# Reordering the first four steps and joining the weights' pieces one step later, in a fused Mamba-2 and cosine-gated feed-forward kernel

## The chip, the cores and the metric

The kernel runs on one core of a Trainium2 chip. The metric is the device time of one execution in microseconds (us), as a median over runs. The program works with five engines: TensorE (PE, matmuls), VectorE (DVE), ScalarE (ACT), GpSimd (POOL) and SyncE (SP, which here only issues DMAs).

## The reference, cut to what matters

```python
# Mamba-2 SSD: batch 4, heads 8, seq 768, head_dim 32, d_state 16
log_a = np.log(np.clip(a, 1e-06, 1.0))
for c in range(nc):
    cum = np.cumsum(la, axis=-1)
    L = np.exp(cum[:, :, :, None] - cum[:, :, None, :]) * causal
    CB = np.einsum('bhin,bhjn->bhij', Cc, Bc)
    y_intra = np.einsum('bhij,bhjd->bhid', CB * L, xc)
    y_inter = np.einsum('bhin,bhnd->bhid', Cc, state) * np.exp(cum)[:, :, :, None]
    y[:, :, sl] = y_intra + y_inter
    Bx = np.einsum('bhjn,bhjd->bhjnd', Bc, xc) * decay_from_j[:, :, :, None, None]
    state = decay_full[:, :, None, None] * state + np.sum(Bx, axis=2)
# feed-forward on the (3072, 256) rows: w_in is 256 x 2048, w_out 2048 x 256
h = x @ w_in
g = h * np.cos(h)
out = g @ w_out
```

## The kernel before, in words

The sequence of 768 is cut into six chunks of 128 tokens (`NC`), and a chunk's rows of all four batches (512) go through the feed-forward in 16 steps (`NF`), one for each 128 columns of h (chunk 0 is cut otherwise, see below). So there are 96 steps n. The schedule is manual: every engine executes its instructions in the order in which the program writes them, and waits are made by semaphores between engines.

**A step** has these parts. `first(n)` (L652): four fp32 products hp = w_in^T y on PE (L665). `wind_k` (L670): ACT rounds hp/2pi to an integer k (L672). `wind_w` (L675): DVE makes w = hp/2pi - k (L678). `gate` (L685): ACT takes the sine of w with a shift of a quarter turn, which is the cosine (L687). `gated` (L689): DVE multiplies with hp, gT = hp cos (L692). `second(n)` (L725): the product with w_out (L736), issued two steps later (`LAG` = 2). From chunk 1 on `second` calls `seven`, which uses seven half products in place of eight (L774) on differences that POOL makes (`differ`, L717 to L720, and once for the weights `differ_w`, L711). hp lies in one of two PSUM buffers (tag "h"), so `first(n)` waits for `gated(n - 2)`. A second pair of larger PSUM buffers (tag "scan", `pair`) serves the inner products g and the sums y of the scan.

**Chunk 0** is worked as two units of 64 tokens (k = 0 and 1), two batches side by side on 64 partitions each (p, s). For unit k: `spread_a` (L340) spreads the decays a over the partitions by matmuls into PSUM, `decays0` (L350) scans them to the decay matrix lam on DVE (L356), `turn_c` and `turn_b` transpose C and B, `inner` (L408) makes C B^T, `weights` (L419) multiplies it by lam (m), `finish0` (L427) makes y (L440 the share of the old state, L449 the new state, L457 the inner share) and ACT copies it to yT (L468, L470). Unit 1 also needs the reach of the old state, `reach0` (L393) and its scan (L398), and the turned C times the reach, `weigh_c` (L402). Steps 0, 2, 4, ... of chunk 0 belong to unit 0, steps 1, 3, 5, ... to unit 1 (`turn_of`): steps 2j and 2j + 1 read the same columns of w_in and the same rows of w_out.

**The weights** come as 64-bit values and are turned to fp32 in 16 pieces, "in" 0 to 7 and "out" 0 to 7; steps 2j and 2j + 1 read in j and out j. `fetch` (L199) loads a piece. `grade` (L217) has ACT take two copies of it (mag L231 and last L229) and POOL clamp one (L232). `join` (L239) has DVE shift (L244) and or (L246) the words and POOL add the last bits into w_in or w_out (L254); only after that add can a product use the piece. The table `piece` (L879) gives the step of each piece: in j at step 2j - 3, out j at step 2j, from step 4 on; the earlier ones are written out in `first_steps`. In the loop (L974) step n grades `piece[n + 1]` and joins `piece[n]`, after w and before gT.

**Behind gT** of steps 4, 6, 8 and 9 DVE runs the scans of chunk 1's decays (`decays`, L512). `chunk1` loads and `clips` (L870, POOL writes the clipped a to two DRAM tensors, a_cut and a_all, from which SP loads `arow` and `along`) prepare chunk 1; SP issues everything of `rest_of_loads` behind the clips' two stores. `add_s1` is POOL's addition to unit 1's state (L485, L487) after step 6.

**The start** (L828 to L860, then `first_steps`, L927) is an order written by hand for the first 11 us and for steps 0 to 3.

Of the kernel before, what the change touches and what calls it, by code (L numbers as in the profile page):

```python
# [25 lines left out]
def kernel(  # L26
# [254 lines left out]
    for r in (slice(NB * H, W), slice(W, P)):  # L281
# [9 lines left out]
                    axis=mybir.AxisListType.X, op=ALU.add)  # L291
    unit = const.tile([P, HH * P + W], FP32, name="unit")
# [12 lines left out]
    def share_a(k, eng, h0, h1):  # L305
        eng.tensor_tensor(out=a0s[k][:, h0:h1],
                          in0=a0z[:, k:k + 1].to_broadcast([P, h1 - h0, W]),
                          in1=mine[:, h0:h1].unsqueeze(2).to_broadcast([P, h1 - h0, W]),
                          op=ALU.mult)

    share_a(0, G, 6, H)
    share_a(0, V, 0, 6)
    G.memset(along1[:, :, 0:1], 0.0)
# [26 lines left out]
    def spread_a(k, p, i=0, n=1, tag="o"):  # L340

        ps = (pair("a_ps")[:, 0] if tag is None else bank([P, 4 * P], "a_ps", tag))
        ps = spread[k, p, i] = ps[:, 0:H * W // n].rearrange("p (h i) -> p h i", i=W)
        for s in range(2):
            b = 2 * s + p
            PE.matmul(ps[s * W:(s + 1) * W], lhsT=those[:, b:b + 1].to_broadcast([P, W]),  # L346
                      rhs=a0s[k][:, i * H // n:(i + 1) * H // n], start=True, stop=True,
                      tile_position=(0, s * W), skip_group_check=True)
# [78 lines left out]
    def finish0(k, between=None):  # L427
# [36 lines left out]
        if between:  # L464
            between()
# [186 lines left out]
    def first(n, between=None):  # L652
        c, f = divmod(n, NF)
        hp[n] = bank([P, TB], "hp", "h")
# [181 lines left out]
    decays0(0, 1, 1, 2)  # L836
    take_c, of_c = turn_c()
    tp_b = bank([P, 4, P], "tp", "o")
    take_b = turn_b(0, tp_b)
    take_c(0)  # L840
    take_b()
    scan_reach = reach0(1)
    scan_reach()
# [4 lines left out]
    spread_a(1, 0, tag="h")  # L848
# [3 lines left out]
    join("in", 0)  # L852
    weigh_c(1, of_c)
    take_s0, _ = finish0(0)
    spread_a(1, 1, tag="o")
    take_b = turn_b(1, tp_b)
    take_b()
    inner(1, 0)
    for p in range(2):
        decays0(1, p)  # L860
# [66 lines left out]
    def first_steps():  # L927

        take_s0()
        first(0, lambda: inner(1, 1))  # L930
        weigh0(1)
        grade("in", 1)
        units_of_decay()
        for q in range(2):
            weights(1, q)
        take_s1, add_s1 = finish0(1, lambda: wind_k(0))
        join("in", 1)
        wind_w(0)
        first(1)
        rest = grade("out", 0, later=True)  # L940
        gate(0)
        rest()
        clips()
        gated(0)
        join("out", 0)
        wind(1)
        first(2)
        rest = grade("in", 2, later=True)
        gate(1)
        take_s1()  # L950
        rest()
        gated(1)
        second(0)
        grade("out", 1)
        join("in", 2)
        wind(2)
        first(3)
        rest = grade("in", 3, later=True)
        gate(2)
        join("out", 1)  # L960
        rest()
        gated(2)
        second(1)
        wind(3)
        rest = grade("out", 2, later=True)
        gate(3)
        join("in", 3)
        rest()
        gated(3)
        return add_s1  # L970
# [3 lines left out]
    for n in range(AHEAD, NC * NF + LAG):  # L974
        c, f = divmod(n, NF)
        if n < NC * NF:
# [9 lines left out]
            rests = []  # L986
            if n + 1 in piece:
                rests.append(grade(*piece[n + 1], later=True))
            gate(n)
            for rest in rests:  # L990
                if rest:
                    rest()
            if n in piece:
                join(*piece[n])
# [3 lines left out]
            if n not in piece and behind:  # L998
                behind.pop(0)()
# [59 lines left out]
```

## Time and profile before

| What | Value |
|---|---|
| median of 9 runs | 375.12 us (374.8 to 378.87) |
| profiled execution: its time / its span | 374.91 us / 373.1 us |
| PE busy | 364.2 us (98%) |
| DVE, ACT, POOL busy | 280.6 (75%), 172.6 (46%), 214.8 us (58%) |
| first product hp 0 / hp 1 / hp 4 starts at | 13.94 / 18.78 / 29.10 us |
| one product of a step in chunk 0 (4 matmuls, 8 records) | 1.73 us from start to start |
| granted PE clock | 1.000 |

Times count from the start of the span. A row of the timeline gives start, length, engine, line, operation, output<-inputs, shapes and a count; in brackets stands how long the engine was idle before it and what it waited for. An fp32 matmul leaves two records, so four matmuls are x8. PEld is PE's load of the stationary operand. Instructions of one engine overlap by about 0.1 us, so a row of 0.69 us takes about 0.6 us from one start to the next. "mag" and "last" are buffers with several uses, and "m" is the name of several scratch tiles.

### The profile page before, as it was taken

Reading aid. Unit: us, or ns where it says so; the run is one execution under the profiler, and the core shown is the slowest. Engines: PE = TensorE matmul, PEld = TensorE weight load, DVE = VectorE, ACT = ScalarE, POOL = GpSimd, SP = SyncE. Lnnn points to the kernel's source line nnn. Section 1 sums busy time; section 2 is a strip of 40 time slices with the busy share of each in tenths; the row PEclk is TensorE's granted clock in tenths of the full one; section 3 lists DMA queues with packets and bytes.
Section 4 is the critical chain, followed back from the end, with each engine's and each line's share of the span. In section 5 each row is a group of like instructions: output and inputs, shape, how many; then the busy total and the mean of one; then the engine's idle time right before and its main releaser. Section 6 shows DMA issues by size and latency. Waiting matters only on the chain.

```text
span 373.1 us, 8681 instructions
## 1 busy us (share of the span) xinstructions
PE 364.2 (98%) x3272; PEld 325.5 (87%) x3272; DVE 280.6 (75%) x470; ACT 172.6 (46%) x293; POOL 214.8 (58%) x334
## 2 busy tenths in 40 slices
PE   8999999999999999999999999999999999999995
PEld 4578887889889899999999999899999989999994
DVE  6869999889699857987858987766887872543643
ACT  3587756444344435344434445433434443444442
POOL 6566865589856347664444683453685353544451
PEclk9999999999999999999999999999999999999999
DMA  9989987316336641745223635211020100010011
GB/s 145 271 245 226 253 215 154 83 25 161 89 83 84 123 109 17 121 119 137 30 41 33 125 97 137 47 22 17 9 35 7 24 7 2 2 28 2 6 25 28
DMA packets 121353, 31.54 MB, mean 85 GB/s; under 512 B 90496, under 2 KB 117216, under 8 KB 121312
## 3 DMA queue, kind: packets, MB, share of 16 engines
q1 hardware_dynamic: 119024, 30.54, 38.2%
q10 hardware_dynamic: 2288, 0.46, 0.6%
q8 instruction: 26, 0.43, 0.5%
q14 instruction: 15, 0.12, 0.1%
HBM read 27.64 MB, written 3.34 MB: 83 GB/s over the span
## 4 chain that ended last, share of the span: by engine, by line
PE 74%; DVE 8%; POOL 6%; SPq 5%; issue 3%; DMA 2%; ACT 2%; POOLq 0%; DVEq 0%; ACTq 0%
PE hp L665 35%; PE o L774 30%; SPq L155 3%; POOL words L711 2%; PE y L604 2%; DVE mag L246 2%; PE g L562 2%; DVE gT L692 1%; PE a_ps L346 1%; DVE lam L512 1%; POOL gd L717 1%; DVE mag L244 1%; DVE w L678 1%; PE y L597 1%; DMA xr<-in_x_dram 1%
## 5 line engine op out<-in xcount | busy, mean ns | idle before, releaser
L665 PE MATMUL hp<-yT,w_in 128*128 128x256 f32 x768 | 184.1, 382 | 2.5 <-DVE gT L692 1.3
L665 PEld LDWEIGHTS hp<-yT,w_in 128*128 128x128 f32 x768 | 139.2, 190 | 22.7 <-issue 4.5
L717 POOL TENSOR_TENSOR gd<-gT 128x256 f32<-128x256 f32 x79 | 59.0, 747 | 99.2 <-DVE gT L692 97.3
L687 ACT ACTIVATE w<-w,quarter 128x512 f32<-128x512 f32 x96 | 69.2, 721 | 76.9 <-DVE w L678 76.9
L672 ACT ACTIVATE k<-hp 128x512 int32<-128x512 f32 x96 | 57.1, 595 | 83.3 <-PE hp L665 83.1
L678 DVE SCALAR_TENSOR_TENSOR w<-hp,k 128x512 f32<-128x512 f32 x96 | 65.4, 681 | 38.4 <-ACT k L672 38.1
L692 DVE TENSOR_TENSOR gT<-hp,w 128x512 f32<-128x512 f32 x96 | 65.2, 679 | 35.9 <-ACT w L687 27.0
L774 PE MATMUL o<-words,gd 128*128 128x128 f32 x474 | 65.8, 275 | 0.0
L774 PEld LDWEIGHTS o<-words,gd 128*128 128x128 f32 x474 | 59.3, 192 | 0.0
L512 DVE TENSOR_TENSOR_SCAN lam<-arow,unit 128x512 f32<-128x512 f32 x40 | 56.4, 1411 | 0.0
L774 PEld LDWEIGHTS o<-w_out,gT 128*128 128x128 f32 x316 | 47.6, 191 | 4.0
L720 POOL TENSOR_TENSOR gd<-gT,gd 128x128 f32<-128x128 f32 x79 | 44.6, 565 | 6.2
L774 PE MATMUL o<-w_out,gT 128*128 128x128 f32 x316 | 48.0, 274 | 0.0
L719 POOL TENSOR_TENSOR gd<-gT,gd 128x128 f32<-128x128 f32 x79 | 44.1, 558 | 6.2
L583 DVE TENSOR_TENSOR m<-g,lam 128x256 f32<-128x256 f32 x80 | 30.9, 415 | 0.5
L774 PE MATMUL o<-w_out,gd 128*128 128x128 f32 x158 | 30.6, 275 | 0.0
L774 PE MATMUL o<-words,gT 128*128 128x128 f32 x158 | 30.5, 275 | 0.0
L736 PE MATMUL o<-w_out,gT 128*128 128x256 f32 x128 | 30.3, 380 | 0.0
L736 PEld LDWEIGHTS o<-w_out,gT 128*128 128x128 f32 x128 | 24.2, 190 | 3.4 <-POOL w_out L254 0.2
L774 PEld LDWEIGHTS o<-w_out,gd 128*128 128x128 f32 x158 | 24.0, 192 | 0.0
L774 PEld LDWEIGHTS o<-words,gT 128*128 128x128 f32 x158 | 24.0, 192 | 0.0
L791 DVE TENSOR_TENSOR sum<-ps,sum 128x256 f32<-128x256 f32 (+1 forms) x27 | 16.7, 645 | 0.6
(108 smaller groups left out, 264.8 us busy)
## 6 DMA issues: line engine op xcount, KB each, us to landing
arow<-a_cut SPq DMA_DIRECT2D x20, 512.0 KB
words<-in_moe_w_in_dram SPq DMA_DIRECT2D x8, 512.0 KB
words<-in_moe_w_out_dram SPq DMA_DIRECT2D x8, 512.0 KB
out_dram<-sum SPq DMA_DIRECT2D x18, 128.0 KB
blocks<-in_B_dram SPq DMA_DIRECT2D x128, 8.0 KB
blocks<-in_C_dram SPq DMA_DIRECT2D x128, 8.0 KB
xr<-in_x_dram SPq DMA_DIRECT2D x14, 128.0 KB
along<-a_all SPq DMA_DIRECT2D x20, 64.0 KB
```

Of the source, the lines that this page charges most:

```text
L512: V.tensor_tensor_scan(out=lam[c, b][:, hs].rearrange("p h i -> p (h i)"), data0=rows_.rearrange("p h i -> p (h i)"), data1=unit[:, b % 2 ...
L583: V.tensor_tensor(out=m_[js, :, :, is_], in0=g_[js, :, :, is_], in1=l_[js, :, :, is_], op=ALU.mult)
L665: PE.matmul(to_[:, e], lhsT=w_in[:, k, fs], rhs=y[:, k], start=(k == 0), stop=(k == KT - 1), skip_group_check=True)
L672: ACT.activation(k, hp[n], AF.Copy, bias=0.25, scale=INV_2PI)
L678: V.scalar_tensor_tensor(out=w, in0=hp[n], scalar=INV_2PI, in1=k, op0=ALU.mult, op1=ALU.subtract)
L687: ACT.activation(cos, cos, AF.Sin, bias=quarter, scale=TWO_PI)
L692: V.tensor_tensor(out=gT[n], in0=hp.pop(n), in1=cos, op=ALU.mult)
L717: G.tensor_tensor(out=d[:, 0:2], in0=g[:, 1:2].to_broadcast([P, 2, P]), in1=g[:, 3::-3], op=ALU.subtract)
L719: G.tensor_tensor(out=d[:, 2], in0=g[:, 0], in1=d[:, 0], op=ALU.subtract)
L720: G.tensor_tensor(out=d[:, 3], in0=g[:, 2], in1=d[:, 2], op=ALU.subtract)
L736: PE.matmul(o[c, u][:, t], lhsT=g[:, 2 * e + t], rhs=w_out[:, 2 * j + e], start=(j == e == t == 0), stop=(j == NJ - 1 and e == 1), skip_gr ...
L774: PE.matmul(at[q], lhsT=a_[q], rhs=w[q], start=(j == 0 and q in starts), stop=(j == NJ - 1), skip_group_check=True)
```

## The change

In the start: `spread_a` uses one product of 128 columns instead of two of 64 (its stationary operand is a copy, `whose`, that DVE makes in two instructions); the first two spread products of unit 1 are made before unit 0's inner products, in halves, and the reach product and scan come after y of unit 0. Unit 1's inner products and weights are all issued before hp 0, and y of unit 1 is made between the two halves of `first(0)`. In `first_steps` hp 2 and hp 3 are taken from the `pair` buffers (tag None), all four first products come ahead of `second(0)`, k and sine of steps 0 and 1 stand together, and grades, joins and clips are interleaved anew. In the loop step n grades `piece[n]` and joins `piece[n - 1]`; step 3's piece, in 3, is graded in `first_steps` and joined in step 4.

```diff
--- before.py
+++ after.py
@@ -289,6 +289,12 @@
                     axis=mybir.AxisListType.X, op=ALU.add)
     V.tensor_reduce(out=those, in_=bh.rearrange("p (b h) -> p b h", b=NB),
                     axis=mybir.AxisListType.X, op=ALU.add)
+    whose = ms[1][:, 0:2 * P].rearrange("p (q s i) -> p q s i", q=2, s=2)
+
+    def whose_of(p):
+        V.tensor_copy(out=whose[:, p], in_=those[:, p::2].unsqueeze(2).to_broadcast([P, 2, W]))
+
+    whose_of(0)
     unit = const.tile([P, HH * P + W], FP32, name="unit")
     unit0 = unit[:, 0:H * W].rearrange("p (h i) -> p h i", h=H)
     for s, eng in enumerate((V, G)):
@@ -310,6 +316,7 @@
 
     share_a(0, G, 6, H)
     share_a(0, V, 0, 6)
+    whose_of(1)
     G.memset(along1[:, :, 0:1], 0.0)
     G.tensor_scalar(out=a0[:, 1], in0=a0[:, 1], **clip)
     for p in range(2):
@@ -341,11 +348,9 @@
 
         ps = (pair("a_ps")[:, 0] if tag is None else bank([P, 4 * P], "a_ps", tag))
         ps = spread[k, p, i] = ps[:, 0:H * W // n].rearrange("p (h i) -> p h i", i=W)
-        for s in range(2):
-            b = 2 * s + p
-            PE.matmul(ps[s * W:(s + 1) * W], lhsT=those[:, b:b + 1].to_broadcast([P, W]),
-                      rhs=a0s[k][:, i * H // n:(i + 1) * H // n], start=True, stop=True,
-                      tile_position=(0, s * W), skip_group_check=True)
+        PE.matmul(ps, lhsT=whose[:, p].rearrange("p s i -> p (s i)"),
+                  rhs=a0s[k][:, i * H // n:(i + 1) * H // n], start=True, stop=True,
+                  skip_group_check=True)
 
     def decays0(k, p, i=0, n=1):
 
@@ -424,7 +429,7 @@
         V.tensor_tensor(out=m, in0=gs[k, q][:, :, 0:2 * P].rearrange("p k (s i) -> p k s i", s=2),
                         in1=l, op=ALU.mult)
 
-    def finish0(k, between=None):
+    def finish0(k):
 
         m, xk = units[k], xrs[k]
         y = [pair("y") for _ in range(2)] if k else [pair("y")]
@@ -461,8 +466,6 @@
         if k == 0:
             yT[0] = two.tile([P, 2, 2, 2 * P], FP32, tag="yT", name="yT")
         t_ = yT[0][:, k]
-        if between:
-            between()
         if k:
             for t in range(2):
                 ACT.copy(out=t_[:, t].rearrange("p (s i) -> p s i", s=2), in_=y[t][:, :, 0:P])
@@ -649,9 +652,9 @@
         c, f = divmod(n, NF)
         return (f % 2, f // 2) if c == 0 else divmod(f, NJ)
 
-    def first(n, between=None):
+    def first(n, between=None, tag="h"):
         c, f = divmod(n, NF)
-        hp[n] = bank([P, TB], "hp", "h")
+        hp[n] = bank([P, TB], "hp", tag) if tag else pair("hp")[:, 0]
 
         u, j = turn_of(n)
         if c == 0:
@@ -834,30 +837,34 @@
         decays0(0, p, i, 2)
     spread_a(0, 1, 1, 2, "h")
     decays0(0, 1, 1, 2)
+    spread_a(1, 0, 0, 2, None)
+    decays0(1, 0, 0, 2)
     take_c, of_c = turn_c()
     tp_b = bank([P, 4, P], "tp", "o")
     take_b = turn_b(0, tp_b)
+    spread_a(1, 0, 1, 2, "h")
+    decays0(1, 0, 1, 2)
     take_c(0)
     take_b()
-    scan_reach = reach0(1)
-    scan_reach()
     weigh0(0)
     grade("in", 0)
     for t in range(2):
         inner(0, t)
-    spread_a(1, 0, tag="h")
+    spread_a(1, 1, tag="h")
     for q in range(2):
         weights(0, q)
     take_c(1)
     join("in", 0)
+    decays0(1, 1)
+    take_s0, _ = finish0(0)
+    take_b = turn_b(1, tp_b)
+    scan_reach = reach0(1)
+    scan_reach()
+    take_b()
+    take_s0()
+    for t in range(2):
+        inner(1, t)
     weigh_c(1, of_c)
-    take_s0, _ = finish0(0)
-    spread_a(1, 1, tag="o")
-    take_b = turn_b(1, tp_b)
-    take_b()
-    inner(1, 0)
-    for p in range(2):
-        decays0(1, p)
 
     la = const.tile([RB, NU, P], FP32, name="la")
     cut = const.tile([RB, NU, P], FP32, name="cut")
@@ -926,46 +933,47 @@
 
     def first_steps():
 
-        take_s0()
-        first(0, lambda: inner(1, 1))
+        grade("in", 1)
         weigh0(1)
-        grade("in", 1)
         units_of_decay()
         for q in range(2):
             weights(1, q)
-        take_s1, add_s1 = finish0(1, lambda: wind_k(0))
+        states_of = []
+        first(0, lambda: states_of.extend(finish0(1)))
+        take_s1, add_s1 = states_of
         join("in", 1)
+        rests = [grade("out", 0, later=True)]
+        wind_k(0)
+        take_s1()
+        rests.pop()()
         wind_w(0)
         first(1)
-        rest = grade("out", 0, later=True)
+        join("out", 0)
+        wind_k(1)
         gate(0)
+        wind_w(1)
+        gate(1)
+        gated(0)
+        gated(1)
+        first(2, tag=None)
+        rests = [grade("in", 2, later=True)]
+        clips()
+        wind_k(2)
+        rests.append(grade("out", 1, later=True))
+        rests.pop(0)()
+        wind_w(2)
+        join("in", 2)
+        first(3, tag=None)
+        gate(2)
+        rests.pop()()
+        join("out", 1)
+        gated(2)
+        second(0)
+        wind(3)
+        rest = grade("in", 3, later=True)
+        gate(3)
         rest()
-        clips()
-        gated(0)
-        join("out", 0)
-        wind(1)
-        first(2)
-        rest = grade("in", 2, later=True)
-        gate(1)
-        take_s1()
-        rest()
-        gated(1)
-        second(0)
-        grade("out", 1)
-        join("in", 2)
-        wind(2)
-        first(3)
-        rest = grade("in", 3, later=True)
-        gate(2)
-        join("out", 1)
-        rest()
-        gated(2)
         second(1)
-        wind(3)
-        rest = grade("out", 2, later=True)
-        gate(3)
-        join("in", 3)
-        rest()
         gated(3)
         return add_s1
 
@@ -983,19 +991,17 @@
             wind(n)
             for at in pairs(n):
                 turn2(*at)
-            rests = []
-            if n + 1 in piece:
-                rests.append(grade(*piece[n + 1], later=True))
+            rest = grade(*piece[n], later=True) if n in piece else None
             gate(n)
-            for rest in rests:
-                if rest:
-                    rest()
-            if n in piece:
-                join(*piece[n])
+            if rest:
+                rest()
+            joins = n - 1 in piece and piece[n - 1] in held
+            if joins:
+                join(*piece[n - 1])
 
             behind = [lambda at=at: halved(*at) for at in halves_at(n)]
             behind = [lambda at=(c, 2 * u + 1): masked(*at) for c, u in pairs(n - 2)] + behind
-            if n not in piece and behind:
+            if not joins and behind:
                 behind.pop(0)()
             gated(n)
             if n == AHEAD + 2:
```

## The prediction

> **What bounds the kernel now.** I read the busy time by stage first, then PE's timeline of the first 60 us, then the instructions of one step, last the chain that ended last. "hp n" is the first product of step n (4 matmuls, 8 records), T(n) its start, "second n" the product with w_out, two steps behind. Columns by stage: busy PE, PEld, DVE, ACT, POOL.
>
> ```profile
> 0.00:11.40 11.40, 9.81 (x160) 5.39 (x160) 7.99 (x21) 4.73 (x10) 6.35 (x20) 1.00 0.95 164
> 11.40:29.10 17.70, 15.97 (x226) 11.54 (x215) 12.65 (x20) 13.00 (x26) 11.96 (x17) 1.00 0.97 253
> 29.10:58.00 28.90, 28.50 (x133) 24.58 (x133) 28.25 (x37) 19.38 (x34) 20.57 (x22) 1.00 0.89 234
> 58.00:373.10 315.10, 309.95 (x2766) 284.00 (x2766) 231.68 (x395) 135.47 (x225) 175.96 (x277) 1.00 0.30 58
> ```
>
> From 29.1 us PE has no room; only the head has (17.70 - 15.97 = 1.7 us idle, besides work that can be moved). But from 29.1 to 58 DVE is just as full (28.25 of 28.90). A gain at the head must get through a stage with two full engines. PE's rows, with the idle time before each:
>
> ```profile
> 11.44 1.08 PE L346 MATMUL a_ps<-m,those 128*64 128x512 f32 x4
> ...
> 13.35 0.67 PE L415 MATMUL g<-cT,turned 32*64 32x128 f32 x16 [0.46 <-ACT turned L391]
> 13.94 1.13 PE L665 MATMUL hp<-yT,w_in 128*128 128x256 f32 x4
> ...
> 18.78 1.99 PE L665 MATMUL hp<-yT,w_in 128*128 128x256 f32 x8 [0.33 <-ACT yT L468]
> 21.05 1.32 PE L665 MATMUL hp<-yT,w_in 128*128 128x256 f32 x5 [0.28 <-DVE gT L692]
> 22.89 0.81 PE L665 MATMUL hp<-yT,w_in 128*128 128x256 f32 x3 [0.52 <-issue]
> ...
> 32.63 1.89 PE L665 MATMUL hp<-yT,w_in 128*128 128x256 f32 x8
> 34.35 1.89 PE L736 MATMUL o<-w_out,gT 128*128 128x256 f32 x8
> 36.08 1.89 PE L665 MATMUL hp<-yT,w_in 128*128 128x256 f32 x8
> 37.81 1.89 PE L736 MATMUL o<-w_out,gT 128*128 128x256 f32 x8
> ...
> 57.96 1.97 PE L665 MATMUL hp<-yT,w_in 128*128 128x256 f32 x8 [0.40 <-DVE gT L692]
> ```
>
> A product takes 1.73 us of PE, a step 3.45. Second 4 (37.81) starts 37.81 - 32.63 = **5.18 us after T(5)**. That is the deadline of a w_out piece joined in step 5 and first read by second 4. How long a join takes is seen in step 4, T(4) = 29.10 (ACT, DVE, POOL rows of the timeline):
>
> ```profile
> 31.10 0.60 ACT L672 ACTIVATE k<-hp 128x512 int32<-128x512 f32 x1 [0.21 <-PE hp L665]
> ...
> 31.73 0.69 DVE L678 SCALAR_TENSOR_TENSOR w<-hp,k 128x512 f32<-128x512 f32 x1
> 32.34 0.42 DVE L244 TENSOR_SCALAR mag<-mag 128x512 uint32<-128x512 uint32 x1
> 32.36 0.86 POOL L232 TENSOR_SCALAR mag<-mag 128x512 f32<-128x512 f32 x1
> ...
> 32.79 0.98 DVE L246 SCALAR_TENSOR_TENSOR mag<-words,mag 128x512 uint32<-128x512 uint32 x1
> ...
> 33.85 1.27 POOL L254 TENSOR_TENSOR w_out<-mag,last 128x512 uint32<-128x512 uint32 x1 [0.63 <-DVE mag L246]
> 34.29 1.91 DVE L512 TENSOR_TENSOR_SCAN lam<-arow,unit 128x512 f32<-128x512 f32 x1
> ```
>
> hp 4 ends, k at T+2.00, w at T+2.63, shift +3.24, or +3.69, add +4.75, piece ready at 33.85 + 1.27 = T+6.02. Before, this piece (out 2) has until 37.81, 2.7 us to spare, because it is joined in its own step. In the chain of waits the stretch from 26.8 to 60 us is almost only DVE's shift, or, gT and scan rows.
>
> [...] So an engine whose next instruction waits holds all that follows; the trace agrees (hp 4 and all behind it waited for gT 2, 28.96 to 29.10). [...] the or (L246) took 0.69 alone (16.80) and 0.98 beside POOL's L232 (32.79). [...] two 512-column products of 64 columns took 1.08 together (11.44), but eight of 256 took 2.89 (3.92), 0.36 each, where one 128x256 product takes 1.73 / 4 = 0.43.
>
> **The change, part by part.**
>
> *Undivided spread products.* Four products of 0.43 = 1.73 take the place of eight (2.89): the first scan starts near 4.7 instead of 5.16, and two more halves (step 1, p 0) follow. But PE then waits for c0 (POOL L323 ends 6.69, transposes at 6.74), which waits for the DMA of C: the 1.1 us is not passed on. On DVE six half scans (0.66 each) end where four and the reach scan ended: the last takes the slot 8.17 to 8.87 of L398. Weights of unit 0 stay at 9.32, y of unit 0 ends near 11.5 as before. whose_of adds two 128x128 copies on DVE, not in the trace; between 0.17 (the 128x128 memset, L79) and 0.41 (a 64x512 copy, L296). I take 0.2: the first lies in the 0.37 wait for a (L299), the second delays only slot and share_a of step 1, wanted near 5.6. Nothing; 0.3 if the cover fails.
>
> *Unit 1.* From 11.44 the two products of 1.01 are gone from PE (one undivided one stands at 9.25, where two stood). Transposes 11.44, reach product 11.9, inner products 12.4 to 13.6 (before 13.35 and 15.0). DVE: scan 11.6, reach 12.8, weights 13.4 and 14.0 (before 14.08, 15.74). First half of hp 0 at 13.6, y of unit 1 from 14.8 (weights end 14.65), 1.8 us (16.66 to 18.45 before), second half at 16.6. hp 1 at 17.5 (18.78). hp 2 and hp 3 lie in y's banks, so no gT is waited for: 19.2 and 20.9; seconds 0 and 1 at 22.7 and 24.4; PE free at 26.1.
>
> *hp 4.* It needs gT 2. Both sines stand together, then comes the mag of in 2 and k of step 2 (22.4 instead of right after hp 2 at 21.2); w 2 at 23.0; join of in 2 to 24.9; then POOL's clips (1.1 us, now behind mag of in 2) hold back out 1's clamp, shift 25.2, or, gT 2 26.5 to 27.1. hp 4 at 27.2 instead of 29.10: **gain 1.9**; 3.0 if DVE kept up (26.1), 1.4 with every contended duration. The clips are issued some 2.8 us later (23.2; 20.35 before), and with them SP's queue: a_cut, a_all, 14 loads of chunk 1, six pieces. arow for the first scan, which had landed near 29, comes near 31.7; wanted at 32.2. Pieces out 3 onward are wanted later still. Nothing, up to 0.5.
>
> *The joins.* From step 4 each step grades its own piece and joins that of the step before. DVE no longer meets POOL's clamp, and has one join (1.3 us) less before each point. For w_in it fits: in j is joined in step 2j-2, needed 6.9 us after T, ready at T+6.0. For w_out it doesn't: **out j is joined in step 2j+1 and needed by second 2j at T+5.18**, ready at T+6.0 plus 0.08. PE then stands 0.9 us in step 2j+2, with everything behind it, and T of the next step moves along, so that the next piece is no better off. One by one, for out 2 to out 7:
> - out 2: the scan (1.91) after gT 4 stands ahead of w 5, which starts about 0.8 late: 1.7.
> - out 3: POOL has add_s1 (42.04 to 44.67) and weigh ahead of the clamp: 1.0.
> - out 4: the scan after gT 8 is absorbed by the former stall: 0.85.
> - out 5: deadline 0.44 later (transposes L540), but reach (1.43, L503) and rT (0.41) ahead: 1.25.
> - out 6: deadline T+5.28 (62.42 to 67.70): 0.8.
> - out 7: T+5.29 (71.35 to 76.64), POOL idle, or alone: 0.6.
>
> Sum 6.2. Low end: uncontended or (0.69) and clamp (0.61), about 0.55 each, with 0.7 for scans 4.0. High end: each 0.3 longer, 7.9. Of before's waits 0.40 (57.96) and 0.1 (53.35) go, as DVE is no longer the later one.
>
> *Sum:* -1.9 - 0.5 + 6.2 = **+3.8 us**. The profiled execution took 374.91 (span 373.1 and 1.8 around it); the median is 375.12, 0.2 above. 375.12 + 3.8 gives 378.9; I say **378.8**.
>
> **Rivals.**
> - *Deadline met: faster.* If w_out's adds end by T+5.18, only the head's gain remains: 1.9 to 3.0, and 0.5: 375.12 - 2.9 = 372.2. For it: DVE is freer, no clamp is awaited. Against: k, w, shift, or, add are 0.6 + 0.6 + 0.45 + 0.7 + 1.27 after T+2.0, at least T+5.7 even alone. The point is a join at least 0.5 shorter than its rows.
> - *Short stalls and full gain: no change.* 4.0 - 3.0 - 0.5 = +0.5: 375.6. For it: fewer collisions of DVE and POOL. Against: POOL's clamp still falls on DVE's or.
> - *Head gain lost as well.* hp 4's chain on DVE or the late loads leave hp 4 at 28.6 or later and the first scan waits: 7.9 - 0.5 - 0.5 = +6.9: 382.0.
> - *The change doesn't do what it says.* The compiled order puts the joins after w of the next step and PE's second 4, 6, ... behind a wait for POOL, so it does.
>
> **How the numbers follow.** A difference of 0.5% (1.9 us) is about what a measurement of this kernel tells from no change. Forecast, stalls 4.5 to 7.9: 0.73. Short stalls and full gain: 0.14. Deadline met: 0.08. Head lost: 0.05. Range 375.9 to 380.9: from near the short-stall case to 7.9 - 1.6 - 0.5 = +5.8. Some of the forecast's lower end lies within 0.5% (0.03). Faster 0.08, same 0.17, slower 0.75.
>
> **What would show it.** In the profile after, waits of PE's L739 for POOL's w_out (L254) must appear, six of 0.5 to 1.8 us, at seconds 4, 6, ... 14 (before, none). hp 1 must start near 17.5 and hp 4 near 27.2. From about 78 us on, all steps must run as before, merely shifted. I am wrong if second 4 follows hp 6 without idle time, or if hp 4 starts at 29 or later.

## The result, and the profile after

The change makes the kernel slower: 381.81 us in the median of 9 runs (380.25 to 383.11) against 375.27 (28 runs of the kernel before, same chip), a ratio of 1.0167 with a 95% interval of 1.0148 to 1.0186, so 6.5 us. The profiled execution, among the slowest of the nine, took 383.04 us with a span of 381.3. The forecast was 378.8, at most 380.9: the direction was right, the size was not.

The stages after, cut at hp 4 as for the kernel before (columns: window; busy PE, PEld, DVE, ACT, POOL with their counts; granted PE clock; DMA share; GB/s):

```profile
11.40:28.06 16.66, 15.63 (x296) 12.81 (x276) 12.63 (x19) 12.01 (x25) 11.77 (x15) 1.00 0.89 237
28.06:58.00 29.94, 25.71 (x108) 21.12 (x107) 24.35 (x32) 16.95 (x28) 17.21 (x18) 0.94 0.85 227
58.00:86.00 28.00, 25.88 (x202) 21.14 (x201) 22.71 (x39) 13.40 (x23) 14.79 (x17) 1.00 0.48 90
86.00:381.30 295.30, 289.89 (x2593) 266.98 (x2591) 214.30 (x364) 125.72 (x208) 165.50 (x265) 1.00 0.28 56
```

Before, PE had 0.4 us without work between 29.1 and 58 us; now it has 4.2, and DVE, which was full, has 5.6. So neither PE nor DVE is short of time any more; something is waited for. The last row says where that ends: 295.30 us with 289.89 of PE, where the same number of instructions (2593) took 295.10 with 289.95 before. All but 0.2 us of the difference arises before 86 us. The second row has one more novelty, a clock of 0.94. PE's timeline after:

```profile
28.06 1.89 PE L668 MATMUL hp<-yT,w_in 128*128 128x256 f32 x8
30.18 1.99 PE L739 MATMUL o<-w_out,gT 128*128 128x256 f32 x8 [0.23 <-POOL w_out L254]
...
35.46 1.89 PE L668 MATMUL hp<-yT,w_in 128*128 128x256 f32 x8
39.92 3.62 PE L739 MATMUL o<-w_out,gT 128*128 128x256 f32 x8 [2.58 <-POOL w_out L254]
43.38 1.89 PE L668 MATMUL hp<-yT,w_in 128*128 128x256 f32 x8
...
49.44 1.99 PE L739 MATMUL o<-w_out,gT 128*128 128x256 f32 x8 [0.71 <-POOL w_out L254]
...
66.05 1.99 PE L739 MATMUL o<-w_out,gT 128*128 128x256 f32 x8 [1.11 <-POOL w_out L254]
```

hp 4 starts 1.04 us earlier than before (29.10). Then the six waits for w_out's add stand where the prediction put them, at seconds 4, 6, ... 14 (2.58, 0.71, 0.71, 1.11, 0.52, 0.49), and one of 0.23 that it didn't have. Step by step the kernel falls behind: hp 6 is 0.62 ahead, hp 7 3.85 behind (43.38 for 39.53), hp 9 4.83, hp 11 5.73, hp 13 6.39, hp 15 7.18, hp 17 7.94, the end 8.2 (spans; the 6.5 of the medians is taken apart below). Almost two thirds of the surprise (8.2 for 3.8) lie between hp 6 and hp 7: the one step costs 4.47 us where 1.7 was forecast. Its parts are the wait, and a second 4 that takes 3.62 in place of 1.89. DVE shows why the wait is long:

```profile
35.39 1.48 DVE L515 TENSOR_TENSOR_SCAN lam<-arow,unit 128x512 f32<-128x512 f32 x1 [0.99 <-DMA arow<-a_cut]
36.80 0.66 DVE L681 SCALAR_TENSOR_TENSOR w<-hp,k 128x512 f32<-128x512 f32 x1
```

The scan behind gT 4 waited 0.99 for arow, and w 5, where the chain of the join begins, came after it. SP issued arow at 28.86 (25.97 before), behind clips that POOL began at 24.02 (20.35 before). The clock, in short windows (columns as above):

```profile
37.20:39.90 2.70, 0.15 (x1) 0.00 (x0) 2.50 (x6) 2.32 (x4) 1.27 (x2) 0.99 0.53 57
39.90:41.60 1.70, 1.68 (x4) 1.41 (x5) 1.67 (x4) 1.29 (x2) 1.07 (x2) 0.50 0.48 73
41.60:43.40 1.80, 1.80 (x6) 1.41 (x6) 1.80 (x2) 0.00 (x0) 1.80 (x2) 0.54 0.70 206
```

After 2.55 us without a matmul PE was granted half its clock, for 3.41 us (39.83 to 43.24). The mean clock of each execution tells that the fall did not always happen. In four of the nine runs the clock was 0.999 or 1.000, and they took 380.25 to 381.39; in five it was 0.995 or 0.996, and they took 381.81 to 383.11. In 3.41 us at half clock PE does the work of 1.7 us (second 4 took 3.46 for 1.73), so that one fall costs 1.7 us and lowers the mean by 1.7/381 = 0.0045, which is just that. So the median of 381.81 holds some 1.3 us of clock (381.81 less 380.54, the middle of the four).

### The profile page after: what moved, and what is told of

Same layout as the page of the kernel before. It is cut to its first block, busy times and chain, and to the rows that moved or that the text cites. A ratio compares the mean times of both kernels' runs of the same rounds, so it can differ in the third digit from the quotient of the medians.

```text
span 381.3 us, 8664 instructions
## 1 busy us (share of the span) xinstructions
PE 366.5 (96%) x3262; PEld 327.9 (86%) x3262; DVE 282.7 (74%) x473; ACT 172.5 (45%) x293; POOL 215.4 (57%) x334
## 3 DMA queue, kind: packets, MB, share of 16 engines
HBM read 27.64 MB, written 3.34 MB: 81 GB/s over the span
## 4 chain that ended last, share of the span: by engine, by line
PE 76%; DVE 7%; POOL 7%; DMA 3%; issue 3%; ACT 2%; SPq 1%; POOLq 0%; DVEq 0%; ACTq 0%
PE hp L668 36%; PE o L777 29%; PE y L607 3%; PE o L739 2%; POOL words L714 2%; PE g L565 2%; DMA arow<-a_cut 2%; DVE mag L246 2%; DMA bc<-in_C_dram 2%; DVE lam L515 1%; POOL w_out L254 1%; PE y L600 1%; POOL gd L720 1%; DVE mag L244 1%; DVE w L681 1%
## 5 line engine op out<-in xcount | busy, mean ns | idle before, releaser
L723 POOL TENSOR_TENSOR gd<-gT,gd 128x128 f32<-128x128 f32 x79 | 45.5, 576 | 6.2
L722 POOL TENSOR_TENSOR gd<-gT,gd 128x128 f32<-128x128 f32 x79 | 44.1, 559 | 6.2
L739 PE MATMUL o<-w_out,gT 128*128 128x256 f32 x128 | 32.4, 400 | 6.4 <-POOL w_out L254 6.4
L254 POOL TENSOR_TENSOR w_out<-mag,last 128x512 uint32<-128x512 uint32 x8 | 10.2, 1270 | 14.5 <-DVE mag L246 14.5
```

What stands on the lines that cost most here:

```text
L722: G.tensor_tensor(out=d[:, 2], in0=g[:, 0], in1=d[:, 0], op=ALU.subtract)
L723: G.tensor_tensor(out=d[:, 3], in0=g[:, 2], in1=d[:, 2], op=ALU.subtract)
L739: PE.matmul(o[c, u][:, t], lhsT=g[:, 2 * e + t], rhs=w_out[:, 2 * j + e], start=(j == e == t == 0), stop=(j == NJ - 1 and e == 1), skip_gr ...
```

## The experiments

Ratios are to the kernel before on the same chip (375.3 to 375.4), with 95% intervals.

**1. The parts alone and paired.** *head_only*: the new start, with before's loop of grades and joins.

```diff
-            rest = grade(*piece[n], later=True) if n in piece else None
+            rests = [grade(*piece[n + 1], later=True)] if n + 1 in piece else []
...
-                join(*piece[n - 1])
+                join(*piece[n])
```

> The changed kernel with the joins in their old steps (each piece joined in its own step, graded one step ahead); the reordered head stays. Theory J (the late joins of w_out's pieces make PE wait, 6.2 us in the changed kernel's second products 4 to 14): all PE waits for POOL's L254 from step 5 on go, and the head's 1.0 us gain at hp 4 is left, or less, as DVE is full again from 30 to 58 us and arow still lands near 35 us: 373.5 to 375.5. Theory C (the clips, 3.7 us later, are the main cost through the late arow): DVE waits for arow some 1 to 2 us with no room to catch up, 376 to 377.5. Theory H (the reordered head itself loses): above 377.5.

Measured 378.29 (376.25 to 380.91), ratio 1.0083 [1.0048, 1.0118]. By its number this is theory H, that the head itself loses; *head_clips_early* below shows that the late clips lose it. *late_joins_only* is the reverse, before's start and clips with the new loop.

> The kernel before with only the loop's grades and joins moved one step later (in 3 joined in step 4, out 2 graded in step 4); the old head and the old clips stay. Theory J: six waits of PE for L254, about 1.2 (second 4, behind the scan), then 0.9, 0.9, 1.2, 0.7, 0.6, in all 5.5, less the 0.5 of waits for gT that go: 379.5 to 380.5. [...] Theory C: arow lands near 30 as in the kernel before, so hardly more than 1 us is lost: 376 to 377.5.

Measured 381.76 (381.49 to 381.95), 1.0173 [1.0158, 1.0188], more than the 379.5 to 380.5 expected. Its first wait (PE's timeline):

```profile
36.63 1.89 PE L665 MATMUL hp<-yT,w_in 128*128 128x256 f32 x8
39.88 2.00 PE L736 MATMUL o<-w_out,gT 128*128 128x256 f32 x8 [1.35 <-POOL w_out L254]
41.71 1.89 PE L665 MATMUL hp<-yT,w_in 128*128 128x256 f32 x8
```

A row is 1.89 long where the next starts 1.73 after it. So second 4, which starts 3.25 after hp 6, is delayed by 1.52, though the listed idle time is 1.35. This delay from start to start is what the prediction priced (T+6.1 for T+5.18). For the six products it is 1.52, 1.05, 0.87, 1.26, 0.68 and 0.66, together 6.04, where 6.2 was forecast. And the product after the wait is slower: second 4 takes 1.83 (39.88 to 41.71) in place of 1.73, and the five others likewise, together another 0.6. With that the six cost 1.62, 1.15, 0.98, 1.37, 0.78 and 0.75, together 6.65. The mean clock was 0.998 or more in all four runs. The joins alone make the kernel as slow as the whole change does (381.76 and 381.81), so the new head brought nothing in the end, though hp 4 came earlier.

*clips_early*: the changed kernel, with the clips issued two steps earlier.

```diff
         wind_w(0)
+        clips()
         first(1)
...
-        clips()
         wind_k(2)
```

> The changed kernel with clips() ahead of the join of out 0 on POOL, where the timeline shows 1.8 us of idle time; nothing else changes. Theory C+J: a_cut is stored some 4 us earlier, arow lands near 31, the scan of step 4 no longer waits (0.99 before), second 4's wait falls from 2.58 to about 1.5, the granted PE clock stays at 1.0 (it fell to 0.5 for 3.4 us after that wait, worth 1.7 us): 378 to 379.3. Also out 1's clamp no longer stands behind the clips, so hp 4 starts up to 0.7 earlier. Theory J alone (clips harmless): 381 to 382.

Measured 380.44 (379.61 to 381.26), 1.0142 [1.0117, 1.0167], between its two theories. hp 4 stands at 27.23, the gain of 1.9 that was forecast; second 4 waits 1.94 in place of 2.58. Here too the mean clock of two runs of four was lower: 379.61 and 379.96 with 1.000, 380.91 and 381.26 with 0.995 and 0.996. *head_clips_early* has both edits: new head, early clips, old joins.

> Both undone: the reordered head with the old joins and with clips() ahead of the join of out 0. Theory J+C: only the head's gain is left, 1.0 to 2.0 us, as far as DVE, full from 30 to 58 us, lets it through: 373.0 to 374.7. If DVE holds it all back: 375. Theory H (the head itself loses): above 375.5.

Measured 374.76 (374.05 to 376.41, 12 runs), 0.9986 [0.9972, 0.9999]: the only complete kernel of this study whose median is under before's, by 0.6 us (375.34), and just above the 373.0 to 374.7 expected. hp 4 is 2.35 us earlier (26.75), but hp 8 only 1.08, hp 10 0.66 and hp 12 0.29; on the way hp products wait for gT, which in the changed kernel they didn't.

**2. Clock and noise.** *after_again* is the changed kernel once more.

> The changed kernel once more, for its spread (380.25 to 383.11 in nine runs) and a second profile. If the fall of the granted PE clock after second 4's wait is by chance of each run [...], this profile may lack it; then [...] the run is 1.7 us or more below 383.1. If it is a fixed part of the change, the profile shows it again. 380.3 to 383.1.

381.79 (380.35 to 382.0), 1.016 [1.0138, 1.0183]. PE's timeline:

```profile
34.78 1.89 PE L668 MATMUL hp<-yT,w_in 128*128 128x256 f32 x8
38.60 2.99 PE L739 MATMUL o<-w_out,gT 128*128 128x256 f32 x8 [1.93 <-POOL w_out L254]
41.39 2.62 PE L668 MATMUL hp<-yT,w_in 128*128 128x256 f32 x8
```

The wait at second 4 was only 1.93 and the clock fell all the same: it was 1.00 from 38.60 to 39.40 and 0.53 in the mean from 39.40 to 43.00, and second 4 and hp 7 took 2.79 and 2.45. In the profile of *clips_early* an equal wait of 1.94 left the mean clock at 1.000, and second 4 took 1.83. So the length of the wait alone doesn't decide; what else does isn't shown. *warm_fill* puts three products that nobody reads ahead of second 4.

```diff
+        if n == AHEAD + 2:
+            fill(pair("warm")[:, 0].rearrange("p (q m) -> p q m", m=P), 3)
         if n >= LAG:
```

> The changed kernel with three idle products (128x512, ones by ones, 0.86 us each, into a spare buffer that nobody reads) ahead of second 4, so that PE is busy while it would wait for out 2. Theory idle-clock (the fall of the granted clock to 0.5 for 3.4 us comes from PE's 2.7 us without work): the clock stays at 1.0, second 4 takes 1.73 instead of 3.46 where it fell, so runs lie near 380 to 381.3 with less spread upwards. Rival (the fall has another cause, such as the DMA load): the fall stays, 381.5 to 383.

380.87 (380.80 to 381.00), 1.0144 [1.0127, 1.0161]. The fill keeps PE busy from 36.91 on, second 4 takes 1.73, no mean clock is below 0.997, and the spread of the runs shrinks from 2.9 to 0.2 us. Without the idle time there is no fall. The median goes down by 0.9; that it isn't the 1.7 of one fall is probably because not all runs of the changed kernel had one, and because the fill takes time itself. The two weren't separated.

**3. w_out on time.** *out_clips_early*: clips early, w_in's pieces late, w_out's pieces joined in their own step as before.

```diff
+            if n % 2 == 0:
+                for m in (n - 1, n):
+                    if m in piece and piece[m] in held:
+                        join(*piece[m])
```

> The reordered head, clips() ahead of the join of out 0, w_in's pieces joined one step later as in the change, but w_out's pieces joined in their own step as before (both joins in the even steps). Theory J (only w_out's deadline costs): all waits of PE for L254 from second 4 on go. And DVE has one join (1.3 us) less ahead of each gT up to step 12, so less of the head's gain is lost to waits for gT than in the kernel with both undone (2.5 us in 6 waits, 374.76): 373.3 to 374.8. If two joins in one step make gT of even steps late (needed 6.9 us after T, ready at 2.6 + 0.6 + 2 x 1.35 + 0.6 = 6.5 and a scan behind it): 375 to 376.5.

381.3 (380.96 to 381.41), 1.0154 [1.0139, 1.0169]: none of the gains expected, and above the rival's 375 to 376.5 too. All waits for w_out from second 4 on are gone, and in their place stand others (waits of PE: us in all, times, the longest):

```profile
PE hp L668 <- DVE gT L695: 7.9, 9, 1.6
```

Two joins now stand in one even step ahead of gT, and the second or runs beside POOL's add (DVE's timeline):

```profile
41.00 0.69 DVE L246 SCALAR_TENSOR_TENSOR mag<-words,mag 128x512 uint32<-128x512 uint32 x1
41.60 0.42 DVE L244 TENSOR_SCALAR mag<-mag 128x512 uint32<-128x512 uint32 x1
42.06 1.64 DVE L246 SCALAR_TENSOR_TENSOR mag<-words,mag 128x512 uint32<-128x512 uint32 x1
```

The same or takes 0.69 alone and 1.64 beside the add; before's timeline had 0.98 beside the clamp. The join's work doesn't vanish, it picks its victim: the product with w_out, or gT.

**4. The spread products.** *divided*: the kernel of 374.76 with before's divided products, without the copies whose.

```diff
-        PE.matmul(ps, lhsT=whose[:, p].rearrange("p s i -> p (s i)"),
+        for s in range(2):
+            PE.matmul(ps[s * W:(s + 1) * W], lhsT=those[:, b:b + 1].to_broadcast([P, W]),
```

> The kernel with old joins and early clips (374.76), but the spread products divided in columns again (two of 64 for each of 128) and without the two copies on DVE. By the prediction's step 'nothing': within 0.4 of 374.8. If the undivided products bring the head's gain: 375.2 or more, with the first scan near 5.2 instead of 4.9 and hp 4 up to 0.8 later.

375.84 (375.44 to 376.88), 1.0016 [1.0007, 1.0025], 1.1 us more than undivided. *divided_again* is its second profile.

> The kernel with the new head, early clips, old joins and divided spread products once more, for its profile. If the 1.8 us that PE stood ahead of hp 2's rows (waiting for nothing that the profile shows) belongs to the divided products, it stands there again and hp 4 starts near 28.6; if it belongs to one execution, it is gone and hp 4 starts near 27.1, 0.2 to 0.4 later than with undivided products.

One run, 377.17. The odd gap stands again (PE's timeline):

```profile
23.73 3.40 PE L668 MATMUL hp<-yT,w_in 128*128 128x256 f32 x15 [2.61 <-issue]
```

It is 1.80 us in the first profile and 2.61 in this one, in the midst of hp 2 and hp 3, and there is none in the undivided kernel of 374.76. But the kernel before has 0.52 at 22.89, and the changed one, which is undivided, 0.60 at 24.39. "issue" means that the profile shows nothing that was waited for. In these four profiles the gap stands ahead of one and the same matmul, the 348th on record, and the divided products, which add 14 matmuls (3276 for 3262), bring that one earlier in the work. What PE stood for isn't shown, and no run varied it alone. The first scan (5.16 for 4.95) accounts for only 0.2 of the 1.1; the gap can account for the rest, an estimate from its length.

**5. DVE as the place where the head's gain goes.** The four scans behind gT 4, 6, 8 and 9 become copies, which leaves out the products of these decays:

```diff
-        V.tensor_tensor_scan(
-            out=lam[c, b][:, hs].rearrange("p h i -> p (h i)"),
+        if c == 1 and b < 2:
+            V.tensor_copy(out=lam[c, b][:, hs].rearrange("p h i -> p (h i)"),
```

*before_copies*:

> The kernel before with the four scans of chunk 1's decays behind gT 4, 6, 8 and 9 (1.91 us each on DVE) replaced by copies of the same 512 columns (left out: the products of these decays, so part of the output is another). Theory, that DVE is full from 30 to 58 us but hidden: only the waits of 0.1 and 0.4 us for gT vanish, so 0.3 to 0.5 us less than before: 374.8 to 375.0. Rival, that the stage doesn't depend on DVE: no difference.

375.81 (374.36 to 378.97), 1.0016 [0.999, 1.0041]: a miss, it isn't lower. *head_copies*:

> The new head with clips early and the old joins, and the same four scans replaced by copies (left out: the products of these decays). Theory, that DVE without room from 30 to 58 us takes the head's gain of 2.35 us back: the six waits of hp products for gT (2.5 us in all) shrink below 0.7, hp 12 comes 2 us or more earlier than before's 57.96, and the time is 372.5 to 373.2, 1.6 to 2.2 below the same kernel with its scans (374.76). Rival, that the collisions of POOL's clamp with DVE's or take it, or w_in's and w_out's joins: the waits stay above 1.5 us and the time is 374.0 to 374.8.

374.22 (371.96 to 377.8, 20 runs), 0.9964 [0.9941, 0.9986]: the time is the rival's, the waits (below) are the theory's. *joins_copies*, the same in *clips_early*:

> The changed kernel with clips early (380.44) and the same four scans replaced by copies (left out: the products of these decays). Theory, that the scan behind gT 4 lengthens the first late join by 1.2 us and the others' waits come from the chain of k, w, shift, or and add alone: the wait at second 4 falls from 1.94 to about 0.7, those at seconds 6 to 14 stay within 0.3 of 0.9, 0.7, 1.1, 0.5 and 0.5, and the time is 379.0 to 379.6. Rival, that the late joins' waits are due to DVE's load: all the waits shrink and the time falls below 377.5.

378.44 (378.21 to 378.72), 1.0078 [1.0054, 1.0101], somewhat below the 379.0 to 379.6 expected. The waits at seconds 4 to 14 are 1.15, 0.71, 0.71, 1.02, 0.52 and 0.49: the scan lengthens the first by 0.8 (1.2 was expected) and hardly the rest, whose cause is the join's own chain.

The first two look alike in the median, and their traces say more. In *head_copies* the waits for gT up to 90 us are all gone, and at 128 us it is 2.5 us ahead of before (hp at 125.64 for 128.12), 1.7 ahead of *before_copies* (127.37; the old head has won 0.75 too). DVE was the taker up to there. Then, at 180 us, both stop for the same thing; in *before_copies* 2.14 us, in *head_copies* 2.22, in *head_only* 1.75. DVE's timeline of *head_only*:

```profile
181.06 0.41 DVE L529 STREAM_TRANSPOSE turned<-blocks 128x256 f32<-128x256 f32 x1
183.22 0.45 DVE L529 STREAM_TRANSPOSE turned<-blocks 128x256 f32<-128x256 f32 x1 [1.75 <-DMA blocks<-in_C_dram]
```

PE stands behind it (1.25 at 184.66, for ACT's cT, which is made from turned). The kernel before made the second transpose of this pair near 180.3 and waited for nothing: just in time. And SP, which loads these blocks in 32 small DMAs, has no gap to catch up (SP's timeline of the kernel before; length is the time of its issues):

```profile
168.47 2.28 SPq L155 DMA_DIRECT2D blocks<-in_B_dram  x4
170.79 2.25 SPq L155 DMA_DIRECT2D blocks<-in_C_dram  x4
173.14 0.42 SPq L164 DMA_DIRECT2D arow<-a_cut  x1
173.61 1.25 SPq L174 DMA_DIRECT2D along<-a_all  x2
174.91 2.50 SPq L155 DMA_DIRECT2D blocks<-in_C_dram  x4
```

From 30 to 176 us the rows of this view sum to 141.6 of 146 us. SP's queue is a third full engine, and the clips' stores lie near its start. Between *head_only* and *head_clips_early*, which differ in the clips alone, the issue of arow is 2.6 us apart (29.06 and 26.46), and the loads of chunk 3's C 150 us later still 2.7 (179.29 and 176.60). Late clips aren't the only way to this lateness: *before_copies*, with its clips unmoved, issued these loads at 177.63, where the kernel before did at 174.91. A part of that is the two issues of x at 50.5 (5.37 for 4.03 together); the rest is open.

**6. SP's queue.** First the four stores of chunk 0's outputs went to ACT's queue, in four kernels.

```diff
-            nc.sync.dma_start(out=unit_rows[p, u], in_=ob[p * W:(p + 1) * W])
+            nc.scalar.dma_start(out=unit_rows[p, u], in_=ob[p * W:(p + 1) * W])
```

> The kernel before, with the four stores of chunk 0's outputs (85.27 to 91.3 us, 3.0 us of issues) on ACT's queue instead of SP's. Theory, that SP's queue (141.6 us of issues between 30 and 176 us) delivers chunk 3's C just in time: no wait at 180 us stands there to be removed, so 374.9 to 375.6, no change. Rival, that the four issues disturb ACT: 376 or more.

> The changed kernel's head with the old joins and late clips (378.29), the four stores on ACT's queue. Theory, that the late clips cost by way of SP's queue, which is 3 to 4 us late until chunk 3's C: the wait of PE at 184.66 (1.25 us) vanishes and 1.6 to 2.0 us with it: 376.1 to 376.9, and the spread of runs (4.7 us) shrinks. Rival, that the loss at 180 us is the transfers' own time and not the queue's: within 0.5 of 378.3.

> The head with early clips and old joins (374.76), the four stores on ACT's queue. Theory: the DMA wait before 180.62 (0.65 us) vanishes and the end comes 0.5 us earlier: 374.0 to 374.4. Rival, DVE alone sets the end: 374.6 to 374.9.

> The same with the four scans of chunk 1's decays behind gT replaced by copies (374.22; left out: the products of these decays). Theory, that DVE from 30 to 58 us and SP's queue at 180 us each take a part of the head's gain: at 128 us it is 2.4 us ahead of before, without the wait of 2.2 us for chunk 3's C it keeps 2.0 or more: 372.0 to 373.0. Rival, another limit behind these two: the gain is lost at a later place and the time stays above 373.6.

Measured 378.38, 380.67, 378.29 and 379.37: 2.4 to 5.1 us slower than the same kernels with the stores on SP (375.3, 378.29, 374.76, 374.22), so the theory's numbers failed in all four; the control's rival, that the issues disturb ACT, is what came. ACT's timeline of *before_stores*:

```profile
79.25 0.57 ACT L742 COPY ob<-o 128x512 f32<-128x512 f32 x1
82.39 1.69 ACTq L744 DMA_DIRECT2D out_dram<-ob  x2
84.12 0.60 ACT L672 ACTIVATE k<-hp 128x512 int32<-128x512 f32 x1 [4.30 <-PE hp L665]
```

The store was issued 2.6 us after its data was copied, and k, behind it on ACT, came 4.3 us after ACT's last work; PE then stood 1.54 us. So ACT, the issuing engine, stood itself. What ended the store's wait isn't listed here, but in two of the three other kernels the profile names it for the k behind the first store: "DMA blocks<-in_C_dram", a load that SP had issued, after 6.40 us without work of ACT in *head_stores* and 8.75 in *head_copies_stores*. Why a store on ACT stands for a load of SP's isn't shown. PE lost so much at 82 us that chunk 3's blocks were never late: nothing was learnt of SP. The second try adds nothing to another engine: the stores are issued on SP after the loads of chunk 3.

```diff
         for p in range(2):
-            nc.sync.dma_start(out=unit_rows[p, u], in_=ob[p * W:(p + 1) * W])
+            unstored.append(lambda p=p: nc.sync.dma_start(out=unit_rows[p, u],
+                                                          in_=ob[p * W:(p + 1) * W]))
...
+        if n == 38:
+            for do in unstored:
+                do()
```

> The changed kernel's head with the old joins and late clips (378.29), the four stores of chunk 0's outputs issued on SP behind the loads of chunk 3 (step 38) instead of at 85 to 95 us; nothing is added to ACT. Theory, that the late clips cost at 180 us by way of SP's queue: with 3 us of issues less ahead of it chunk 3's C comes before it is wanted, PE's wait of 1.25 us at 184.66 vanishes and 1.6 to 2.0 us with it: 376.1 to 376.9. Rival, that C's lateness isn't the queue's: the wait stays and the time is within 0.5 of 378.3.

*head_later*: 375.4 (374.81 to 376.22, 14 runs), 0.9994 [0.9977, 1.0012], against 378.29 with the stores in their old place. The wait is gone (DVE's timeline, both transposes in one row):

```profile
180.72 0.74 DVE L529 STREAM_TRANSPOSE turned<-blocks 128x256 f32<-128x256 f32 x2
```

Expected were 376.1 to 376.9. The gain of 2.9 is more than the wait because three of the six runs of *head_only* also had a mean clock of 0.995 or less (378.89 to 380.91) and none of *head_later* had; against the three others (middle 376.98) it is 1.6.

> The head with early clips and old joins and with the four scans of chunk 1's decays behind gT replaced by copies (374.22; left out: the products of these decays), the four stores issued behind the loads of chunk 3. Theory, that DVE from 30 to 58 us and SP's queue at 180 us each take a part of the head's gain: without both it is kept, 372.0 to 373.0. Rival, another limit behind these two: above 373.6.

*head_copies_later*: 372.37 (372.16 to 372.74), 0.9908 [0.9876, 0.9941], as expected. With DVE relieved from 30 to 58 us and SP at 180 us the head's gain reaches the end, and the spread is 0.6 us where *head_copies* had 5.8. The 3.0 us below before (375.37) are more than the 2.35 at hp 4. The old head with both reliefs was not run; as *before_copies* was 0.75 ahead at 128 us, some 0.7 of the 3.0 may not be the head's.

## Why the prediction failed, point by point

With the executions in which the clock did not fall, each term of the sum can be set beside a measured part. Late joins alone: 381.76 - 375.34 = +6.4 (forecast 6.2 - 0.5 = 5.7). New head on top, clips early: 379.79 (two runs) - 381.76 = -2.0 (forecast -1.9). Clips late: 380.54 - 379.79 = +0.8 (forecast 0). The clock, in the median: 381.81 - 380.54 = +1.3 (no term). These are neighbours in one chain, so that they must come to +6.5 together; what they show is where the 2.7 us lie that the forecast of 3.8 lacks: 1.3 with the clock, 0.8 with the clips, 0.7 with the joins, and nothing with the head.

- **The failed step: "PE then stands 0.9 us ... and T of the next step moves along", with every product behind it priced at 1.73.** That PE stands, where, and how long was right: 6.04 us of delay for 6.2. The sum took the delay to be all that a stall costs and had no term for what it does to the products after it. In the profile after, second 4 took 3.46 (39.92 to 43.38) in place of 1.73, because the granted clock fell to 0.50 after the wait. Such a fall costs 1.7 us, came in five of nine executions, and is worth 1.3 in the median, the largest of the missing parts; *warm_fill*, where PE has no idle time there, has no fall (mean clock 0.997 to 1.000). Without a fall too the product after a wait took 1.83 for 1.73, in all six 0.6 us (*late_joins_only*).
- **The joins, nearly right in size.** Mechanism and places were right, all six. The terms 1.7, 1.0, 0.85, 1.25, 0.8 and 0.6 came as 1.52, 1.05, 0.87, 1.26, 0.68 and 0.66. Of the 0.7 by which 6.4 is over 5.7, the slower products are 0.6, and the delays take 0.2 off; 0.3 isn't assigned.
- **The clips: "Nothing, up to 0.5".** Wrong. arow was forecast to come near 31.7 and wanted at 32.2. It was there for a scan at 35.39 that could have started at 34.40. The issue was 2.9 us late as forecast, but from issue to use it then took 6.5 us. With late joins this cost 0.8 (two runs against four: not well resolved). With the old joins it costs far more, 378.29 against 374.76, at a place 150 us later that the prediction didn't look at: "Pieces out 3 onward are wanted later still" asked for the next users of SP's queue and not for where the queue ends.
- **The head: right in size, by luck.** 1.9 was forecast for hp 4; it is 1.9 in *clips_early*, 2.0 in *after_again* (27.08) and 1.0 in the profile after. But the reason, "It needs gT 2", is not what held hp 4. hp 2 and hp 3 lie in y's banks, as the prediction says itself, so hp 4 goes into hp 0's buffer and needs only gT 0. In *clips_early* it started at 27.23, before DVE began gT 2 at 27.64 (in the profile after 28.06 and 28.63). It was PE's own stream that held it (PE's timeline of *clips_early*):

```profile
17.60 6.31 PE L668 MATMUL hp<-yT,w_in 128*128 128x256 f32 x28
27.23 1.99 PE L668 MATMUL hp<-yT,w_in 128*128 128x256 f32 x8
```

The first row is the second half of hp 0 with hp 1, 2 and 3, without a pause. hp 1 began near 18.5 where 17.5 was forecast, and seconds 0 and 1, behind this row, ended at 27.2 where PE was to be free at 26.1. A PE that is 1.1 late and a wait for gT 2 that doesn't come cancel in the number. In the profile after hp 4 stands 0.8 later still. There C's DMA landed later (transposes at 7.47, 6.92 in *clips_early*), and PE's stream has the "issue" gap of 0.60. Neither is a fixed part of the change: in five traces with this start the transposes stand at 6.92 to 7.62, and *after_again* has its reach product at 11.70 (12.44 in the profile after) and no such gap. That a gain at the head has to pass "a stage with two full engines" was right: without the late joins 2.35 us became 0.3 at hp 12. Three full queues, it should have said.

- **The spread products: "Nothing".** The copies whose took 0.58 and 0.47 in the profile after, not 0.2, and undividing brings 1.1 us (375.84 to 374.76). That isn't because products get shorter. The prediction set 0.36 for a product of 64 columns against 0.43 for one of 128, as if the halves hardly ran side by side. In the profile of before the matmuls of two halves start within 0.01 us of each other, and two of 512 columns took together (1.08) what one undivided takes (PE's timeline after):

```profile
3.78 3.27 PE L351 MATMUL a_ps<-m 128*128 128x256 f32 x10
9.98 1.12 PE L351 MATMUL a_ps<-m 128*128 128x512 f32 x2
```

The 0.36 were long because they came early. Up to 5.7 us one record of a matmul followed the other every 0.43 us, divided or not, and later every 0.22 (an undivided product has two records); the first row is such a mixture. The same five products took 2.97 in *head_clips_early* and 4.00 in *head_later*. What undividing brings is then not in the products; the "issue" gap of experiment 4 can explain it.

- **The rivals.** "Head gain lost as well" gave 382.0, nearest to the result, and the first scan did wait as it said; but hp 4 was not late. The number came out for half of its reason. "Deadline met" is refuted by six waits, "doesn't do what it says" too. "Short stalls" is refuted by delays of 6.04 in all where it had 4.0.

Open are what, beside the length of a wait, makes the clock fall, what else made SP's queue late in *before_copies*, how much of the 3.0 us of *head_copies_later* is the head's, what PE stands for in the "issue" gap, why a store on ACT stands for a load of SP's, and 0.3 us of the joins.

## What to carry to other kernels

Price a wait on the bounding engine as the delay of the next start, add what the product after it loses (0.10 us here), and ask for each wait what the clock does after it (here it fell after 2.55 and 1.93 us). When a forecast number comes true, still look at what ended the wait: hp 4 came when it should have, for another reason. When issues are moved on a DMA queue, sum the queue's own rows: if they fill the time, a delay at its start can arrive undiminished (2.6 and 2.7 us here) at the last transfer that is due just in time, however far away. A gain made ahead of a full stage is worth only what every full queue behind it lets through (2.35 us became 0.3 at hp 12 here); relieve them one by one and look where it is lost next.

## What the runs showed of the hardware

- The granted clock fell to 0.50 for 3.41 us after 2.55 us without matmuls, and in another execution after 1.93 (*after_again*), while an equal wait of 1.94 left it at 1.000 (*clips_early*); of nine executions of the same program five had a mean clock 0.004 lower and took 1.8 us more (382.38 and 380.54, the middles of the two groups).
- The product after a wait of PE took 1.83 in place of 1.73, without any fall of the clock (*late_joins_only*, mean clock 1.000).
- Two products of 64 columns each ran side by side: 1.08 for a pair of 512 (kernel before, 11.44), 1.12 for one undivided of 128 columns (changed kernel, 9.98).
- A gap of PE at 22 to 24 us, listed as "issue", stood ahead of the 348th matmul on record in four profiles: 0.52 us in the kernel before, 0.60 in the changed one, 1.80 and 2.61 in the two of *divided*.
- One DVE instruction of 128x512 words (the or) took 0.69 alone (kernel before, 16.80), 0.98 beside POOL's clamp (the same, 32.79) and 1.64 beside POOL's add of two operands (*out_clips_early*, 42.06).
- SP's issues of blocks of 8 KB took 0.58 us each, back to back (4.62 for eight, kernel before, 72.94), so that 32 of them are 18 us of queue.
- A store issued on ACT went out 2.6 us after its data was ready, and ACT's next work, behind it, came 4.3 us after the last (*before_stores*); in *head_stores*, where this took 6.40, the profile names a load that SP had issued as what ended it.
